# Loading 384 depthwise weights straight to their partitions, and the first two supertiles' transposes and stores in another order

## The chip, the cores and the metric

The kernel runs on one core of one Trainium2 chip. The metric is the device time of one execution in microseconds; the time before is 574.61 us, the median of 7 runs (574.41 to 575.1). A NeuronCore has engines with instruction streams of their own: TensorE (PE in the profile, with PEld for the loading of the stationary operand), VectorE (DVE), ScalarE (ACT), GpSimd (POOL) and SyncE (SP), which here only issues DMAs. Sixteen DMA engines move data between HBM and the on-chip SBUF. Engines wait for each other, and for DMAs, by semaphores.

## The reference

With k = 1 the depthwise part is a scaling of each of the 384 channels, and the pointwise part a 384 x 384 matrix product on each of the 384 x 384 pixels:

```python
xp = jnp.pad(x, ((0,0),(pad,pad),(pad,pad),(0,0)))       # pad = 0
for i in range(k):
    for j in range(k):
        out = out + xp[:, i:i+H, j:j+W, :] * dw[i, j][None, None, None, :]
return jnp.einsum('bhwc,cd->bhwd', out, pw)
```

Inputs and output are bf16: x is (1, 384, 384, 384), dw (1, 1, 384), pw (384, 384). 147,456 pixels of 768 bytes are read and as many written.

## The kernel before

The scaling is folded into the matrix: row c of pw is multiplied by dw[c] once, and then out = x times the scaled matrix. A supertile is 512 pixels, and there are 288 of them. They are loaded in chunks: 1, 1, 2, 2 and 4 supertiles (group 0), then groups of 10, and smaller chunks again at the end. Three X buffers and three O buffers hold a group each and are used in turn.

For each supertile VectorE makes two transposes (L349, halves h = 0 and 1) of 32 x 32 blocks of pairs of bf16, from X into T. TensorE multiplies (L211): 48 matmuls in 12 steps of four, one for each group of 32 rows of the array, into one of two PSUM halves PS[0], PS[1]. ScalarE copies PSUM to O as bf16 (L406), and SP stores O. T, PS and O are guarded by the semaphores s_t, s_pe, s_a and s_o. TensorE runs the supertiles in a hardware loop (L270); the last supertile has code of its own.

Before the loop the scaled matrix w_r is made in the layout that the transposes leave. Each step of it has a line:

- ScalarE's queue loads dw as one row in one partition (L166, dw_row). SP's queue loads pw in two DMAs (L167, L168), and then x: the chunks of group 0, then groups 1 and 2 (L128). Group 1's load is issued after supertile 1's has landed.
- TensorE works on constants meanwhile (`idle_work`, L228: four groups of four matmuls, and two more groups after dw). Three small matmuls (L241) turn dw_row into a column for each third of the channels, in PSUM; VectorE copies them to dw_f (L374).
- GpSimd makes an identity matrix, VectorE adds it up to a selection matrix sel (L367), and multiplies sel by each column of dw_f (L377), which gives sel_w for k = 0, 1, 2.
- TensorE multiplies sel_w with pw (L261), six results (k, r); it waits for the first pw DMA, for the second at k = 1, and for each sel_w. The results are copied to w_r (L362): number 1 by VectorE, the others by ScalarE in order.
- The first matmul of the loop waits for number 1, for ScalarE's first three casts and for the first transpose; two later steps of the first supertile wait for the fourth and the fifth cast (`w_first`).
- On VectorE the order is: sel, dw_f, the three sel_w, its cast of w_r, the four transposes of supertiles 0 and 1, and then the loop, in which the transposes of supertile jj + 2 follow the eviction of jj.

SP's stream is a list sorted by due times (`todo`): a load of a group that reuses an X buffer is due after the last supertile of the group that had it, and a store one place after the supertile it ends with. Each group-0 chunk has one store. Ahead of the very first store stand 28 waits that are already satisfied (L183). A store waits for ScalarE's copy, then its DMA is issued (L161). ScalarE waits for the stores of a group before its O buffer is written again (L390).

The transposes write T by the pattern below, so that the word at place i*4 + k of T is row i of block k. The pixel of output partition p is then p itself, and a chunk's store writes, for each of the four row groups q, L*768 contiguous bytes a partition.

```python
Tw = Ts[s][:].bitcast(U32).rearrange("p b (i k) -> p b k i", k=4)
```

Of the kernel before, what the change touches and what calls it, by code (L numbers as in the profile page):

```python
# [7 lines left out]
BF16 = mybir.dt.bfloat16  # L8
F32 = mybir.dt.float32
U32 = mybir.dt.uint32  # L10
# [3 lines left out]
NR = 3  # L14
LONG_AT = [8, 148]
PARTS = [slice(0, 4, 2), slice(1, 2), slice(3, 4)]
# [11 lines left out]
def kernel(  # L28
# [12 lines left out]
    nc = tc.nc  # L41
    P = nc.NUM_PARTITIONS
    B, H, W, C = x.shape
    assert dw.shape[0] == 1 and dw.shape[1] == 1, "only k=1 depthwise supported"
    D = pw.shape[1]
# [7 lines left out]
    NS = N // 512  # L53
    groups = _groups(NS)

    chunks, first = [], 0
# [2 lines left out]
            chunks.append((g, i, sum(ls[:i]), first, L))  # L59
            first += L  # L60
    NT = len(chunks)
    n_parts = [1 if c[0] + 1 < len(groups) else len(PARTS) if c[3] + 1 == NS else 2 for c in chunks]
    g_end = [max(c[3] + c[4] for c in chunks if c[0] == g) - 1 for g in range(len(groups))]

    consts = ctx.enter_context(tc.tile_pool(name="consts", bufs=1))
# [7 lines left out]
    eye = consts.tile([P, P], BF16, name="eye")  # L73
    sel = consts.tile([P, 2, 32], F32, name="sel")
    w_r = consts.tile([P, NB, 2, D], BF16, name="w_r")
    dw_row = consts.tile([1, C], BF16, name="dw_row")
    dw_f = consts.tile([P, 3], F32, name="dw_f")
    warm = consts.tile([P, 2], F32, name="warm")

    ones = nc.const_aps.tensor(1.0, [P, D], BF16)  # L80
# [17 lines left out]
    s_dw = nc.alloc_semaphore("s_dw")  # L98
    s_pw = nc.alloc_semaphore("s_pw")
    s_pw2 = nc.alloc_semaphore("s_pw2")  # L100
    s_df = nc.alloc_semaphore("s_df")
    s_sw = nc.alloc_semaphore("s_sw")
    s_dwf = nc.alloc_semaphore("s_dwf")
    s_sel = nc.alloc_semaphore("s_sel")
# [3 lines left out]
    with tc.tile_critical(sync_engine=mybir.EngineType.Pool, no_gpsimd_drain=True):  # L108
# [25 lines left out]
        def store(t, k):  # L134
            g, i, off, first, L = chunks[t]
            je = first + L * (k + 1) // n_parts[t] - 1
            src = Os[g % NR][:, 4 * off * D : 4 * (off + L) * D]
            rows = of[512 * first : 512 * (first + L), :]
            if first + 2 < NS:
                dst = rows.rearrange("(q p j) d -> p q (j d)", q=4, p=P)  # L140
                src = src.rearrange("p (q e) -> p q e", q=4)
                e = L * D // n_parts[t]
                dst, src = dst[:, :, e * k : e * k + e], src[:, :, e * k : e * k + e]
                nc.sync.wait_ge(s_a[je % 2], je // 2 + 2)
            elif first + 2 == NS:
                dst = rows.rearrange("(m q) d -> m (q d)", q=4)
                part = slice(2 * D * k, 2 * D * k + 2 * D)
                dst, src = dst[:, part], src[:, part]
                nc.sync.wait_ge(*((s_a[0], NS // 2 + 1) if k == 0 else (s_d, 1)))
            else:  # L150
                dst = rows.rearrange("(m p) d -> p m d", p=P)[:, PARTS[k], :]
                src = src.rearrange("p (m d) -> p m d", d=D)[:, PARTS[k], :]
                if k == 0:
                    nc.sync.wait_ge(s_d, 2)
                    nc.sync.wait_ge(s_a[1], NS // 2 + 1)
                elif k == 1:
                    nc.sync.wait_ge(s_d, 3)
                else:
                    nc.scalar.wait_ge(s_a[1], NS // 2 + 2)
            eng = nc.scalar if first + 1 == NS and k == 2 else nc.sync  # L160
            eng.dma_start(dst, src).then_inc(s_o[g % NR], 16)  # L161
# [1 line left out]
        w_eng = [1, 0, 1, 1, 1, 1]  # L163
        w_all = [(s_wr[e], w_eng.count(e)) for e in range(2)]

        nc.scalar.dma_start(dw_row[:], dw.rearrange("a e c -> a (e c)")).then_inc(s_dw, 16)  # L166
        nc.sync.dma_start(pw_n[:, 0], pw[0:P, :]).then_inc(s_pw, 16)  # L167
        nc.sync.dma_start(pw_n[:, 1:3], pw[P:C, :].rearrange("(k p) d -> p k d", p=P)).then_inc(s_pw2, 16)  # L168
        load_x(0)
# [7 lines left out]
        for _, f, a in sorted(todo, key=lambda a: a[0]):  # L177
            if f is load_x and chunks[a[0]][4] == LMAX and chunks[a[0]][0] == 1:
                nc.sync.wait_ge(x_of(1)[1], 16)
            if f is store and a[0] == 0:  # L180

                for _ in range(28):
                    nc.sync.wait_ge(s_pw, 16)  # L183
            f(*a)
# [40 lines left out]
        def idle_work(n):  # L225
            for _ in range(n):
                for i in range(4):
                    nc.tensor.matmul(  # L228
                        PS[0][:, 2 * (i % 2) + i // 2, :D],
                        lhsT=ones[32 * i : 32 * i + 32, 0:P],  # L230
                        rhs=ones[32 * i : 32 * i + 32, :],
                        start=True,
                        stop=True,
                        tile_position=(32 * i, 0),
                    )

        idle_work(4)

        nc.tensor.wait_ge(s_dw, 16)
        for k in range(3):  # L240
            mm = nc.tensor.matmul(  # L241
                PS[1][:, 0, D + k : D + k + 1],
                lhsT=dw_row[:, P * k : P * k + P],
                rhs=ones[0:1, 0:1],
                start=True,
                stop=True,
            )
        mm.then_inc(s_df)
        idle_work(2)
        nc.tensor.wait_ge(s_pw, 16)  # L250
        times = {(2, 0): 2, (2, 1): 2}
        for k in range(3):
# [77 lines left out]
        def transposes(t, j):  # L330
            g, i, off, first, L = chunks[t]
            jj = first + j
            s = jj % 2
            if jj + 1 == NS:
                nc.vector.wait_ge(s_xk, 32)
                Tw = Ts[s][:].bitcast(U32).rearrange("p (v j) (m w) -> p v j m w", v=2, m=4)
                Xw = Xk[:].bitcast(U32).rearrange("p (j v m) w -> p v j m w", v=2, m=4)
                for v in range(2):
                    ins = nc.vector.transpose(out=Tw[:, v], in_=Xw[:, v])  # L339
                    ins._wait_ge(s_pe, 2 * (jj - 2) + v + 1)  # L340
                    ins.then_inc(s_t[s][v])
                return
            X, sem, n = x_of(t)
            Xw = X.bitcast(U32).rearrange("p (k l) c -> p k l c", l=L)
            Tw = Ts[s][:].bitcast(U32).rearrange("p b (i k) -> p b k i", k=4)
            for h in range(2):
                if h == 0 and j == 0:
                    nc.vector.wait_ge(sem, n)
                ins = nc.vector.transpose(  # L349
                    out=Tw[:, 3 * h : 3 * h + 3],  # L350
                    in_=Xw[:, :, j, 96 * h : 96 * h + 96].rearrange("p k (b w) -> p b k w", w=32),
                )
                if jj >= 2:
                    ins._wait_ge(s_pe, 2 * (jj - 2) + h + 1)
                ins.then_inc(s_t[s][h])

        order = [(t, j) for t in range(NT) for j in range(chunks[t][4])]

# [11 lines left out]
            op=mybir.AluOpType.add,  # L370
            axis=mybir.AxisListType.X,
        ).then_inc(s_dwf)
        nc.vector.wait_ge(s_df, 1)
        nc.vector.tensor_copy(dw_f[:], PS[1][:, 0, D : D + 3]).then_inc(s_dwf)  # L374
        nc.vector.wait_ge(s_dwf, 2)
        for k in range(3):
            nc.vector.tensor_scalar_mul(  # L377
                sel_w[:, k], sel[:].unsqueeze(2).to_broadcast([P, 2, 4, 32]), dw_f[:, k : k + 1]
            ).then_inc(s_sw)
        for i in range(6):  # L380
            w_out(i)
# [3 lines left out]
        for jj, (t, j) in enumerate(order):  # L385
            g, i, off, first, L = chunks[t]
            s = jj % 2
            Ov = Os[g % NR][:, 4 * off * D : 4 * (off + L) * D].rearrange("p (q j d) -> p q j d", q=4, d=D)
            if j == 0 and i == 0 and g >= NR:
                nc.scalar.wait_ge(s_o[g % NR], 16 * sum(map(len, groups[g % NR : g : NR])))  # L390
            if jj + 2 == NS:
                nc.vector.wait_ge(s_pe, 2 * jj + 2)
                nc.vector.wait_ge(s_o[g % NR], 16 * sum(map(len, groups[g % NR : g : NR])))
                a = nc.scalar.copy(Ov[:, 0:2, j, :], PS[s][:, 0:2, :D])  # L394
                a._wait_ge(s_pe, 2 * jj + 2)
                a.then_inc(s_a[s])
                nc.vector.tensor_copy(Ov[:, 2:4, j, :], PS[s][:, 2:4, :D]).then_inc(s_d)  # L397
                continue
            if jj + 1 == NS:
                for n, m in enumerate((0, 2, 1, 3)):  # L400
                    o = (nc.scalar.copy if n % 2 else nc.vector.tensor_copy)(Ov[:, m, j, :], PS[s][:, m, :D])  # L401
                    o._wait_ge(s_pe, 2 * jj + 1 + n)
                    o.then_inc(s_a[s] if n % 2 else s_d)
                store(t, 2)
                continue
            a = nc.scalar.copy(Ov[:, :, j, :], PS[s][:, :, :D])  # L406
            a._wait_ge(s_pe, 2 * jj + 2)
            a.then_inc(s_a[s])

            if jj == LONG_AT[0]:  # L410
                load_last(nc.scalar)
            if jj == LONG_AT[1]:
                nc.scalar.wait_ge(s_xk, 32)
                load_x(NT - 2, nc.scalar)
            if jj + 2 < NS:
                transposes(*order[jj + 2])
# [30 lines left out]
```

## Time and profile before

| What | Value |
|---|---|
| median of 7 runs | 574.61 us |
| the profiled execution's own time | 574.66 us |
| its span in the profile | 572.4 us |
| TensorE busy | 566.4 us (99%) |
| VectorE busy | 506.4 us (88%) |
| ScalarE busy | 418.5 us (73%) |
| DMA, mean over the span | 396 GB/s |
| first matmul of the loop (L211) | 6.54 us |
| end of the loop's matmuls | 566.38 us |

Times in the profile count from the start of the span. A line of the timeline has the start, the length, the engine, the line of the kernel, the operation, what it writes and reads, how many instructions are merged into it, and in brackets how long the engine was idle before and what ended that. A wait for several semaphores is put down to one of them, the one that the profile takes to have come last. The loop's matmuls run four at a time, so that their lengths overlap.

### The profile page before, as it was taken

How to read it: one execution, taken by the hardware profiler on the slowest of the kernel's cores; microseconds unless marked ns; L12 is line 12 of the kernel's file. 1: busy time of each engine (PE TensorE's matmuls, PEld its weight loads, DVE VectorE, ACT ScalarE, POOL GpSimd, SP SyncE). 2: the span in 40 equal slices, each digit the busy share in tenths (PEclk: the TensorE clock that was granted, in tenths of full speed). 3: DMA queues.
4: the chain of work that ended last, by engine and by line, in shares of the span. 5: the costliest groups of instructions: out<-in, count | busy, mean ns of one | idle time of the engine just before them, and what ended most of it. 6: DMA issues, size and time to landing. Idle time of an engine off the chain costs nothing.

```text
span 572.4 us, 29681 instructions
## 1 busy us (share of the span) xinstructions
PE 566.4 (99%) x13835; PEld 419.5 (73%) x13835; DVE 506.4 (88%) x585; ACT 418.5 (73%) x297; POOL 17.0 (3%) x45
## 2 busy tenths in 40 slices
PE   8999999999999999999999999999999999999997
PEld 4777777777777777777777777777777777777774
DVE  7889889889889889889888988988988988988985
ACT  6777777777777777777777777777777777777775
POOL 4042000000000000000000000000000000000000
PEclk9999999999999999999999999999999999999999
DMA  8999999999999999999999999999999999999677
GB/s 335 439 387 424 421 421 426 440 419 418 426 418 420 382 397 430 401 379 398 425 389 392 414 421 389 412 413 421 410 383 428 401 391 394 422 394 379 256 289 251
DMA packets 26896, 226.88 MB, mean 396 GB/s; under 512 B 1285, under 2 KB 7558, under 8 KB 23046
## 3 DMA queue, kind: packets, MB, share of 16 engines
q1 hardware_dynamic: 25696, 225.91, 97.4%
q10 hardware_dynamic: 1190, 0.89, 0.5%
q14 instruction: 9, 0.07, 0.0%
q8 instruction: 1, 0.02, 0.0%
HBM read 113.54 MB, written 113.25 MB: 396 GB/s over the span
## 4 chain that ended last, share of the span: by engine, by line
PE 98%; DMA 1%; DVE 0%; SPq 0%; issue 0%; ACT 0%; POOLq 0%
PE ps L211 98%; DMA X<-in_x_dram 1%; PE ps L279 0%; DVE T L349 0%; ACT O L401 0%; SPq L168 0%; SPq L167 0%; SPq L442 0%; POOLq L108 0%; POOLq L431 0%
## 5 line engine op out<-in xcount | busy, mean ns | idle before, releaser
L211 PE MATMUL ps<-w_r,T 32*128 32x384 bf16 x13776 | 559.8, 321 | 0.8 <-DVE T L349 0.8
L349 DVE STREAM_TRANSPOSE T<-X 128x384 uint32<-128x384 uint32 x572 | 499.2, 876 | 57.1 <-DMA X<-in_x_dram 2.1
L211 PEld LDWEIGHTS ps<-w_r,T 32*128 32x128 bf16 x13776 | 417.2, 93 | 143.4 <-issue 1.2
L406 ACT CAST O<-ps 128x1536 bf16<-128x1536 f32 x286 | 411.6, 1439 | 146.8 <-PE ps L211 146.8
L326 POOL COPY Xk<-Xl 32x256 bf16<-32x256 bf16 (+1 forms) x32 | 10.1, 341 | 22.7 <-DMA Xl<-in_x_dram 21.9
L316 POOL COPY raw<-w_r 32x768 bf16<-32x768 bf16 x8 | 6.4, 821 | 6.5 <-ACT w_r L362 6.3
L362 ACT CAST w_r<-ps 128x768 bf16<-128x768 f32 x5 | 3.7, 810 | 0.8 <-PE ps L261 0.8
L228 PE MATMUL ps<-const-bfloat16-1.0 32*128 32x384 bf16 x24 | 2.2, 516 | 1.1 <-PEq L431 1.1
L261 PE MATMUL ps<-raw 64*128 64x384 bf16 x16 | 2.2, 374 | 0.2
L328 ACT ACT_TABLE_LOAD x1 | 1.3, 1283 | 1.5 <-PEq L431 1.5
L279 PE MATMUL ps<-raw,T 64*128 64x384 bf16 (+1 forms) x16 | 2.2, 326 | 0.0
L397 DVE CAST O<-ps 128x768 bf16<-128x768 f32 x1 | 1.0, 956 | 1.4 <-PE ps L211 1.4
L261 PEld LDWEIGHTS ps<-raw 64*128 64x128 bf16 x16 | 0.5, 99 | 2.2 <-DMA raw<-in_pw_dram 1.5
L349 DVE STREAM_TRANSPOSE T<-Xl 128x384 uint32<-128x384 uint32 x2 | 1.8, 877 | 0.2
L279 PEld LDWEIGHTS ps<-raw,T 64*128 64x128 bf16 (+1 forms) x16 | 1.0, 96 | 1.2 <-issue 0.6
L228 PEld LDWEIGHTS ps<-const-bfloat16-1.0 32*128 32x128 bf16 x24 | 0.7, 117 | 1.4 <-issue 1.4
L401 ACT CAST O<-ps 128x384 bf16<-128x384 f32 x2 | 1.0, 479 | 0.9 <-PE ps L279 0.9
L339 DVE STREAM_TRANSPOSE T<-Xk 128x384 uint32<-128x384 uint32 x2 | 1.2, 578 | 0.5 <-PE ps L211 0.4
L367 DVE TENSOR_REDUCE sel<-eye 128x64 f32<-128x128 bf16 x1 | 0.3, 287 | 1.5 <-POOL eye L302 1.5
L401 DVE CAST O<-ps 128x384 bf16<-128x384 f32 x2 | 1.1, 558 | 0.3 <-PE ps L279 0.2
L362 DVE CAST w_r<-ps 128x768 bf16<-128x768 f32 x1 | 1.0, 958 | 0.5 <-PE ps L261 0.5
L394 ACT CAST O<-ps 128x768 bf16<-128x768 f32 x1 | 0.8, 799 | 0.5 <-PE ps L211 0.5
(10 smaller groups left out, 2.5 us busy)
## 6 DMA issues: line engine op xcount, KB each, us to landing
X<-in_x_dram SPq DMA_DIRECT2D x26, 3840.0 KB, 22.0
out_dram<-O SPq DMA_DIRECT2D x26, 3840.0 KB, 28.0
X<-in_x_dram SPq DMA_DIRECT2D x3, 1536.0 KB, 18.8
out_dram<-O SPq DMA_DIRECT2D x4, 768.0 KB, 9.4
out_dram<-O SPq DMA_DIRECT2D x2, 1536.0 KB, 14.1
X<-in_x_dram SPq DMA_DIRECT2D x3, 768.0 KB, 7.5
X<-in_x_dram SPq DMA_DIRECT2D x1, 2304.0 KB, 20.4
out_dram<-O SPq DMA_DIRECT2D x1, 2304.0 KB, 12.2
```

Of the source, the lines that this page charges most:

```text
L211: mm = nc.tensor.matmul(PS[s][:, q, :D], lhsT=Ts[s][32 * q : 32 * q + 32, b, par::2], rhs=w_r[32 * q : 32 * q + 32, b, par, :], start=(b, ...
L228: nc.tensor.matmul(PS[0][:, 2 * (i % 2) + i // 2, :D], lhsT=ones[32 * i : 32 * i + 32, 0:P], rhs=ones[32 * i : 32 * i + 32, :], start=True ...
L261: mm = nc.tensor.matmul(PS[(k + 1) % 2][:, 2 * r + v, :D], lhsT=sel_w[64 * v : 64 * v + 64, k, r, :, :].rearrange("p q w -> p (q w)"), rhs ...
L279: return nc.tensor.matmul(PS[1][:, m, :D], lhsT=Tk[rows, at : at + P, par], rhs=w_k[rows, k, par, :], start=start, stop=stop, tile_positio ...
L316: nc.gpsimd.tensor_copy(w_k[rows, k], w_r[rows, b]).then_inc(s_wk)
L326: nc.gpsimd.tensor_copy(dst, src).then_inc(s_xk)
L328: nc.scalar.copy(warm[:, s : s + 1], nc.const_aps.tensor(0.0, [P, 1], F32)).then_inc(s_a[s])
L339: ins = nc.vector.transpose(out=Tw[:, v], in_=Xw[:, v])
L349: ins = nc.vector.transpose(out=Tw[:, 3 * h : 3 * h + 3], in_=Xw[:, :, j, 96 * h : 96 * h + 96].rearrange("p k (b w) -> p b k w", w=32),)
L362: o = nc.vector.tensor_copy(out, in_) if e == 0 else nc.scalar.copy(out, in_)
L401: o = (nc.scalar.copy if n % 2 else nc.vector.tensor_copy)(Ov[:, m, j, :], PS[s][:, m, :D])
L406: a = nc.scalar.copy(Ov[:, :, j, :], PS[s][:, :, :D])
```

## The change

dw is loaded by a DMA of 384 packets of two bytes, from ScalarE's queue as before, to 128 partitions of three elements (dw_c). The row, the three matmuls, dw_f and their semaphore go; sel_w is now a product of two tensors, sel and dw_c, and VectorE waits for the DMA itself. TensorE's work on constants is five groups in one piece in place of four and two.

The first two chunks, one supertile each, are transposed so that T holds the 32 words of a block k in a run. Output partition p = 32k + i then holds pixel 4i + k of each row group q, so each of these two chunks is stored by four DMAs of 32 partitions. The number of stores in a group enters the waits for O buffers, which are now counted from `n_parts`.

```diff
-    n_parts = [1 if c[0] + 1 < len(groups) else len(PARTS) if c[3] + 1 == NS else 2 for c in chunks]
+    n_parts = [(4 if t < 2 else 1) if c[0] + 1 < len(groups) else len(PARTS) if c[3] + 1 == NS else 2 for t, c in enumerate(chunks)]
...
-    dw_row = consts.tile([1, C], BF16, name="dw_row")
-    dw_f = consts.tile([P, 3], F32, name="dw_f")
+    dw_c = consts.tile([P, 3], BF16, name="dw_c")
...
-            if first + 2 < NS:
+            if t < 2:
+                dst = rows.rearrange("(q i k) d -> k i q d", q=4, k=4)[k]
+                src = src[32 * k : 32 * k + 32].rearrange("p (q d) -> p q d", q=4)
+                if k == 0:
+                    nc.sync.wait_ge(s_a[first % 2], first // 2 + 2)
+            elif first + 2 < NS:
...
-        nc.scalar.dma_start(dw_row[:], dw.rearrange("a e c -> a (e c)")).then_inc(s_dw, 16)
+        with nc.allow_non_contiguous_dma(reason="dw to partitions"):
+            nc.scalar.dma_start(dw_c[:], dw.rearrange("a e (k p) -> p (a e k)", p=P)).then_inc(s_dw, 16)
...
-            if f is store and a[0] == 0:
+            if f is store and a == (0, 0):
...
-        idle_work(4)
-
-        nc.tensor.wait_ge(s_dw, 16)
-        for k in range(3):
-            mm = nc.tensor.matmul(
-                PS[1][:, 0, D + k : D + k + 1],
-                lhsT=dw_row[:, P * k : P * k + P],
-                rhs=ones[0:1, 0:1],
-                start=True,
-                stop=True,
-            )
-        mm.then_inc(s_df)
-        idle_work(2)
+        idle_work(5)
...
-            Tw = Ts[s][:].bitcast(U32).rearrange("p b (i k) -> p b k i", k=4)
+            Tw = Ts[s][:].bitcast(U32).rearrange(
+                "p b (k i) -> p b k i" if t < 2 else "p b (i k) -> p b k i", k=4
+            )
...
+        def o_free(g):
+            return 16 * sum(n_parts[t] for t, c in enumerate(chunks) if c[0] < g and c[0] % NR == g % NR)
...
-        nc.vector.wait_ge(s_df, 1)
-        nc.vector.tensor_copy(dw_f[:], PS[1][:, 0, D : D + 3]).then_inc(s_dwf)
-        nc.vector.wait_ge(s_dwf, 2)
+        nc.vector.wait_ge(s_dwf, 1)
+        nc.vector.wait_ge(s_dw, 16)
         for k in range(3):
-            nc.vector.tensor_scalar_mul(
-                sel_w[:, k], sel[:].unsqueeze(2).to_broadcast([P, 2, 4, 32]), dw_f[:, k : k + 1]
+            nc.vector.tensor_tensor(
+                out=sel_w[:, k],
+                in0=sel[:].unsqueeze(2).to_broadcast([P, 2, 4, 32]),
+                in1=dw_c[:, k : k + 1].unsqueeze(2).unsqueeze(3).to_broadcast([P, 2, 4, 32]),
+                op=mybir.AluOpType.mult,
             ).then_inc(s_sw)
...
-                nc.scalar.wait_ge(s_o[g % NR], 16 * sum(map(len, groups[g % NR : g : NR])))
+                nc.scalar.wait_ge(s_o[g % NR], o_free(g))
```

More of the change, by code (lines that the diff above doesn't have):

```diff
@@ L100 @@
     s_pw2 = nc.alloc_semaphore("s_pw2")
-    s_df = nc.alloc_semaphore("s_df")
     s_sw = nc.alloc_semaphore("s_sw")
@@ L389 @@
             if j == 0 and i == 0 and g >= NR:
-                nc.scalar.wait_ge(s_o[g % NR], 16 * sum(map(len, groups[g % NR : g : NR])))
+                nc.scalar.wait_ge(s_o[g % NR], o_free(g))
             if jj + 2 == NS:
                 nc.vector.wait_ge(s_pe, 2 * jj + 2)
-                nc.vector.wait_ge(s_o[g % NR], 16 * sum(map(len, groups[g % NR : g : NR])))
+                nc.vector.wait_ge(s_o[g % NR], o_free(g))
                 a = nc.scalar.copy(Ov[:, 0:2, j, :], PS[s][:, 0:2, :D])
```

## The prediction

> **What bounds the kernel now.** I read the page first, then the chain that ended last, then the timeline of the first 13 us, then the waits of the DMA queue SP.
>
> The page's first part and its chain by engine:
>
> ```profile
> span 572.4 us, 29681 instructions
> PE 566.4 (99%) x13835; PEld 419.5 (73%) x13835; DVE 506.4 (88%) x585; ACT 418.5 (73%) x297; POOL 17.0 (3%) x45
> ...
> PE 98%; DMA 1%; DVE 0%; SPq 0%; issue 0%; ACT 0%; POOLq 0%
> ```
>
> TensorE is busy 99% of the span and carries 98% of the chain. The chain in order of time says where the rest lies:
>
> ```profile
> 1.87 3.69 DMA X<-in_x_dram
> 5.56 0.02 issue
> 5.59 0.87 DVE T L349
> 6.45 0.09 issue
> 6.54 559.83 PE ps L211 x13776
> ```
>
> From 6.54 us on there is one unbroken run of matmuls: 287 supertiles in 559.83 us, 1.951 us each. Nothing in the change touches a matmul of L211, so the change can move the end in two ways only: it moves the start at 6.54 us, or it makes the run stall. Two chains meet at that start, and the timeline of the first microseconds shows both:
>
> ```profile
> 0.97 0.54 ACTq L166 DMA_DIRECT2D dw_row<-in_dw_dram  x1
> ...
> 2.31 0.21 PEld L241 LDWEIGHTS ps<-const-bfloat16-1.0,dw_row 1*128 1x128 bf16 x2 [0.41 <-DMA dw_row<-in_dw_dram]
> ...
> 2.67 0.16 DVE L374 COPY dw_f<-ps 128x3 f32<-128x3 f32 x1 [0.91 <-PE ps L241]
> ...
> 2.87 0.88 DVE L377 TENSOR_SCALAR raw<-sel,dw_f 128x256 bf16<-128x256 f32 x3
> 3.34 0.16 PEld L261 LDWEIGHTS ps<-raw 64*128 64x128 bf16 x4 [0.74 <-DMA raw<-in_pw_dram]
> ...
> 3.91 3.67 ACT L362 CAST w_r<-ps 128x768 bf16<-128x768 f32 x5 [0.79 <-PE ps L261]
> ...
> 4.26 0.13 PEld L261 LDWEIGHTS ps<-raw 64*128 64x128 bf16 x4 [0.77 <-DMA raw<-in_pw_dram]
> ...
> 5.59 2.95 DVE L349 STREAM_TRANSPOSE T<-X 128x384 uint32<-128x384 uint32 x4 [0.40 <-DMA X<-in_x_dram]
> ```
>
> The data chain: x lands at 5.57, the first transpose ends at 6.45, matmuls start at 6.54. The weight chain: dw lands at 2.27, three tiny matmuls and a copy turn it, sel_w is ready from 3.22 (2.87 plus one L377 of 0.35), L261 starts at 3.34, ScalarE casts from 3.91. The wait at 3.34 is labelled with pw, but pw's first block landed 2.0 us after its issue at 0.96, so at about 3.0; the late one is sel_w. The first supertile needs ScalarE's third cast. It begins at 5.36 and lasts 0.80: 6.17. In the semaphore records TensorE passes the weights at 6.21 and T at 6.49. So the data chain decides, and the weight chain has 0.28 us to spare. Its middle is also held by the second pw block: landed 4.22, seen at 4.26, 0.40 later the second cast.
>
> **The change part by part, against the profiled execution's own time of 574.66 us (0.05 over the median 574.61 of the runs shown).**
>
> *Transposes of supertiles 0 and 1 in contiguous runs.* L349 writes with a stride of four words and takes 0.86 us; L339 at the end of the kernel moves the same 128x384 words in contiguous runs and takes 0.578. I take that row: 0.28 us off each of four transposes. Only the first is on the path: the data chain is ready at 6.545 - 0.28 = 6.27. Bounds: 0 (the runs don't matter) and 0.28. When this goes, the weights are late next: third cast 6.17 plus the same 0.10 to the matmul is 6.27 as well. No more than 0.28 us can be won, and only with unchanged weights.
>
> *dw straight to partitions.* Removed: three L241 matmuls, the L374 copy and two semaphore hops, 2.27 to 2.87. Added: the L377 products become tensor-tensor operations of the same 256 elements; I price them at L377's own 0.35 each (bounds 0.29, the reduction at L367, and 0.58, the contiguous transpose of 384). VectorE now waits for dw itself; behind that wait stand sel_w, one cast of w_r and the first transposes, so a late dw delays all of them and, through sel_w, TensorE and ScalarE. With dw landing at D: product starts D+0.03, ends D+0.38; L261 starts 0.12 later, at D+0.50; the first cast follows 0.57 later (3.34 to 3.91), at D+1.07; ScalarE's casts follow each other at 0.69 to 0.70 (4.67, 5.36), so the third ends 2.19 after the first begins, at D+3.26; plus 0.10, matmuls start at D+3.36. Against 6.545 that breaks even at D = 3.19.
>
> What is D? Before, one packet of 768 B landed 1.30 us after the issue at 0.97. Now 384 packets of 2 B, 24 for each of 16 DMA engines. No row has such a packet. From below: the trace's 4-byte semaphore packets take 9 ns, 24 of them 0.2 us, so D = 2.5. From above: pw's second block, 16 packets per engine of 768 B, landed 1.2 us after the first block, 76 ns a packet; 24 of those are 1.8 us, D = 4.1; and if pw's own 24 packets per engine (36 ns each in the packet records, 0.86 us) come in between, D = 4.95. They will: dw stays on ScalarE's queue, pw and x are on SP's, and at 32 to 33 us, where both queues carry 768 B packets, the records show 159 of the one to 144 of the other, one for one. I take 48 packets of 36 ns from the first packet at 1.94, which is 3.67, plus 0.2 for the landing: D = 3.85. That is near the row of equal packet count, and takes 2 B as no cheaper than 768 B. Then matmuls start at 7.21.
>
> The Trainium skill (DMA: Bandwidth & Descriptors, Specifications) speaks against this edit: under 512 B a DMA engine does a read-modify-write. No row here shows one. As an estimate, if that doubled each packet's 36 ns, D would be 4.7 and the total 576.2; the number below does without it.
>
> *What dw's packets take from the others.* At most 24 x 36 ns = 0.86 us of each DMA engine before x. Between 2 and 3.5 us the engines are half idle (129 to 369 GB/s in the slices of the DMA view there), so I put half on x and pw: x lands at about 6.0, data chain 6.7; pw's second block 4.65, weights 6.7 by that limb. Both are below 7.21. Bounds 0 and 0.86: even 0.86 gives 7.13.
>
> *Idle matmuls, 24 to 20.* Nothing waits for them; they end near 2.9 where sel_w now comes at 4.2. The gap matters only for the clock (rival below).
>
> *Stores of supertiles 0 and 1, 2 DMAs to 8.* Six more issues on SP at 0.40 (10.26 and 12.14 took that), 2.4 us between 10.3 and 13.8, while SP otherwise waits for ScalarE. Queued behind: the next store, whose issue hangs anyway,
>
> ```profile
> 16.04 17.22 SPq L161 DMA_DIRECT2D out_dram<-O  x2
> ...
> 33.30 1.38 SPq L128 DMA_DIRECT2D X<-in_x_dram  x1
> ```
>
> and the x load of group 3, issued at 33.30 and landed at 50.4, first needed at 6.54 + 28 x 1.951 = 61.2. I cost this at nothing; its cover is 10.8 us on the load and, for the O buffers of group 0 (last landing 54.2, wanted at 67), 12.8. Even if each quarter took as long as a whole store did in the queue (1.0 us for the first, 1.9 for the second), that would be 3 x 2.9 = 8.7 us. The tightest place elsewhere is group 1's load: VectorE sees it at 24.35, its transpose ends 25.29, TensorE wants it at 26.04. A delay of x by 0.43 against a start later by 0.67 loosens that.
>
> *Sum.* 7.21 - 6.545 = +0.67 on 574.66: 575.3 in a profiled execution, and about the same against the median, 574.61 + 0.67 = 575.3. A change under 0.2%, 1.15 us, is about what a measurement of this kernel can't tell from none.
>
> **The rivals.**
>
> *A. dw lands early, not slower.* If small packets are nearer 9 ns than 36, D stays at or below 3.19 and the contiguous transposes count: 574.66 - 0.28 = 574.4. For it: 768 B packets keep the engines half idle at 2 to 3.5 us, so there is room. Against: D must beat a load that needed 3.26 us for the same packet count.
>
> *B. dw packets cost more than 768 B ones.* From D = 4.33 on the loss exceeds 1.15 us. At D = 4.95 it is 8.31 - 6.545 = 1.77: 576.4. For it: one packet per element, 24 deep on each engine. Against: the same packets would then delay pw, which the estimate already holds.
>
> *C. The clock comes late.* L228's matmuls take 0.52 us, as do the first of L261; at 4.27 they take 0.36, later 0.32: full speed is granted near 4.35, after 3.2 us of almost unbroken work. Now TensorE idles from 2.9 to 4.35. If the grant comes one such stretch later, at 7.7, L261 and 0.5 us of L211 run at about half speed: +0.6 on top, 575.9. If two later, some 4 us of L211 do, +2: 577.3. Against: a gap of 0.8 us before 6.54 costs no clock.
>
> The Trainium skill (TensorE: Matmul & The Clock Gate, Part 1) gives a free-running window of about 3.4 us whose activity decides the clock; it leaves open how much work in it is enough, so it allows both, and the run will show.
>
> *D. The stores bite.* If the eight small stores held SP or the queue more than 10.8 us longer, group 3 would come late; with double my upper 8.7 that is a stall of 6.6: about 582.
>
> **How the numbers follow.** The likeliest, dw between 3.19 and 4.33: 0.40; A 0.18; B 0.23; C 0.13; D 0.06. Predicted is the likeliest's 575.3; its own range is 574.6 to 575.8. The range for 8 in 10 takes in A's 574.3 and all but the far ends of B and C: 574.3 to 576.8. Slower by over 0.2%: all of B, 0.12 of C, 0.05 of D and 0.01 of the edge, 0.41. Faster by over 0.2% would need matmuls at 5.4, before x lands at 5.57: 0.02 for what I don't see. The same: 0.57.
>
> **What would show it.** In the changed kernel: four transposes near 0.58; the products' start, which is D; L261 0.47 after it; the matmul run starting 3.33 after the products' start and lasting 559.8. If the wait before L211 is on T and not on w_r, A is right. If L261 after 4.4 still shows 0.52, C. If a stall of VectorE on X appears near 61, D. I am wrong if the run starts outside 6.2 to 8.8, or lasts longer than before.

## The result and the profile after

The changed kernel takes 576.44 us, the median of 14 runs (575.59 to 577.0), against 574.61 (34 runs): slower by the ratio 1.0028, 95% interval [1.0021, 1.0035]. The profiled execution took 576.31 us with a span of 574.1, so 1.65 us over the profiled execution of before.

The page's first lines and the chain by engine:

```profile
span 574.1 us, 29673 instructions
PE 567.6 (99%) x13828; PEld 357.1 (62%) x13828; DVE 507.1 (88%) x584; ACT 418.5 (73%) x297; POOL 17.0 (3%) x45
...
PE 99%; DMA 1%; issue 0%; ACT 0%; DVE 0%; POOLq 0%; ACTq 0%; DVEq 0%
```

TensorE is the bound as before. The chain that ended last, in order of time (start, length, what), shows what now stands ahead of the run of matmuls:

```profile
0.97 2.92 DMA dw_c<-in_dw_dram
...
3.99 0.44 DVE raw L373
4.43 0.14 issue
4.56 1.46 PE ps L253 x8
6.03 0.02 issue
6.05 1.47 PE ps L253 x8
7.51 560.71 PE ps L215 x13181
```

Before, this chain began with x and the first transpose. Now it begins with dw, which lands 2.92 us after its issue, and runs through the products and the making of w_r. The timeline of the first microseconds has the same steps and one thing that the chain hides:

```profile
3.99 1.09 DVE L373 TENSOR_TENSOR raw<-sel,dw_c 128x256 bf16<-128x256 f32 x3 [2.23 <-DMA dw_c<-in_dw_dram]
...
4.56 2.95 PE L253 MATMUL ps<-raw 64*128 64x384 bf16 x16 [1.66 <-DVE raw L373]
...
5.10 3.61 ACT L359 CAST w_r<-ps 128x768 bf16<-128x768 f32 x5 [2.05 <-PE ps L253]
...
7.45 5.83 PE L215 MATMUL ps<-w_r,T 32*128 32x384 bf16 x116
...
9.02 0.16 PEld L215 LDWEIGHTS ps<-w_r,T 32*128 32x128 bf16 x4 [0.16 <-issue]
9.34 3.71 PEld L215 LDWEIGHTS ps<-w_r,T 32*128 32x128 bf16 x92 [0.16 <-issue]
```

The first matmul of the loop starts at 7.45 us, 0.91 later than before. And up to 9.34 TensorE loads four weights every 0.32 us; from there on the loads follow without a break. That is the moment when full speed is granted; the trace's clock record has it at 9.40, where before it was 4.35, ahead of the loop. The loop's matmuls last 560.77 us from the first start to the last end, against 559.83. So 0.91 of late start and 0.94 of slow start make 1.84 at the last matmul (568.22 against 566.38), of which the span shows 1.6, since the part behind the last matmul is 0.2 shorter in this execution.

The waits of SP's queue show the load of group 3 and the stores:

```profile
12.10 21.84 SPq L164 DMA_DIRECT2D out_dram<-O  x10
33.98 1.98 SPq L126 DMA_DIRECT2D X<-in_x_dram  x1
```

The ten stores fill the time in which SP hung before anyway, and group 3's load is issued at 33.98 in place of 33.30. It lands at 51.8 and is wanted near 62; VectorE waits for no x after group 0's chunks.

### The profile page after: what moved, and what is told of

Same layout as the page of the kernel before. It is cut to its first block, busy times and chain, and to the rows that moved or that the text cites. A ratio compares the mean times of both kernels' runs of the same rounds, so it can differ in the third digit from the quotient of the medians.

```text
span 574.1 us, 29673 instructions
## 1 busy us (share of the span) xinstructions
PE 567.6 (99%) x13828; PEld 357.1 (62%) x13828; DVE 507.1 (88%) x584; ACT 418.5 (73%) x297; POOL 17.0 (3%) x45
## 4 chain that ended last, share of the span: by engine, by line
PE 99%; DMA 1%; issue 0%; ACT 0%; DVE 0%; POOLq 0%; ACTq 0%; DVEq 0%
PE ps L215 98%; PE ps L253 1%; DMA dw_c<-in_dw_dram 1%; PE ps L271 0%; ACT O L400 0%; DVE raw L373 0%; ACTq L441 0%; POOLq L106 0%; DVEq L371 0%; POOLq L430 0%
## 5 line engine op out<-in xcount | busy, mean ns | idle before, releaser
L215 PEld LDWEIGHTS ps<-w_r,T 32*128 32x128 bf16 x13776 | 354.6, 93 | 206.4 <-issue 1.6
L253 PE MATMUL ps<-raw 64*128 64x384 bf16 x16 | 2.9, 513 | 1.7 <-DVE raw L373 1.7
L253 PEld LDWEIGHTS ps<-raw 64*128 64x128 bf16 x16 | 0.9, 113 | 3.7 <-issue 3.0
```

Of the source, the lines that this page charges most:

```text
L215: mm = nc.tensor.matmul(PS[s][:, q, :D], lhsT=Ts[s][32 * q : 32 * q + 32, b, par::2], rhs=w_r[32 * q : 32 * q + 32, b, par, :], start=(b, ...
L253: mm = nc.tensor.matmul(PS[(k + 1) % 2][:, 2 * r + v, :D], lhsT=sel_w[64 * v : 64 * v + 64, k, r, :, :].rearrange("p q w -> p (q w)"), rhs ...
```

## The experiments

After the result the theory was: the late dw packets delay the weights (0.91 us), the gap in TensorE's work that they leave delays the clock (0.94), and the stores and transposes cost nothing. Rivals: the stores or transposes carry part of it; the clock moves by itself; and, later, several theories on why dw is late. In all runs the head of the kernel was read from the profile, since the times of one kernel spread by 1 to 4 us and their medians alone tell little. The table has, from each trace, when dw, pw's second block and the first x land, the loop's first matmul, the clock's grant (the moment from which the trace shows full speed) and the length of the run of matmuls, and the fastest of the timed runs (the medians are in the text).

| kernel | dw | pw 2nd | x | start | grant | run | fastest |
|---|---|---|---|---|---|---|---|
| before | 2.27 | 4.22 | 5.56 | 6.54 | 4.35 | 559.83 | 574.26 |
| changed | 3.89 | 4.93 | 5.94 | 7.45 | 9.40 | 560.77 | 575.59 |
| e1, dw as a row | 2.24 | 3.97 | 5.45 | 6.25 | 6.65 | 560.00 | 574.21 |
| e2, dw part alone | 3.79 | 4.76 | 5.92 | 7.35 | 9.81 | 561.02 | 575.52 |
| e3, gap filled | 3.92 | 4.74 | 5.84 | 7.48 | 6.92 | 559.83 | 575.29 |
| e4, before with a gap | 2.27 | 3.90 | 5.71 | 6.70 | 7.99 | 560.44 | 574.70 |
| e5, packets unused | 2.55 | 3.94 | 6.42 | 7.41 | 4.61 | 559.83 | 575.20 |
| e6, stores alone | 2.24 | 4.55 | 5.89 | 6.87 | 10.25 | 561.47 | 574.30 |
| e7, a third of dw | 4.02 | 4.86 | 6.06 | 7.58 | 7.82 | 559.93 | 575.44 |
| e8, e1 again | 2.51 | 3.87 | 5.49 | 6.41 | 5.94 | 559.83 | 574.14 |
| e9, 128 x 768 B | 3.41 | 3.96 | 6.19 | 6.97 | 7.64 | 560.14 | 574.91 |
| e10, on SP's queue | 3.61 | 4.80 | 6.55 | 7.25 | 8.22 | 560.28 | 575.39 |
| e11, 128 x 2 B, spread | 3.17 | 5.14 | 6.14 | 7.37 | 10.51 | 561.35 | 574.71 |
| e12, 384 x 2 B, spread | 3.66 | 4.48 | 5.59 | 7.22 | 9.36 | 560.86 | 574.92 |

**e1 and e8: dw as a row, the rest of the change kept.**

```diff
-            nc.scalar.dma_start(dw_c[:], dw.rearrange("a e (k p) -> p (a e k)", p=P)).then_inc(s_dw, 16)
+        nc.scalar.dma_start(dw_row[:], dw.rearrange("a e c -> a (e c)")).then_inc(s_dw, 16)
...
-        idle_work(5)
+        idle_work(4)
+
+        nc.tensor.wait_ge(s_dw, 16)
...
+        mm.then_inc(s_df)
+        idle_work(2)
```

The three small matmuls, the copy to dw_f and the products with a scalar for each partition come back with it.

> The changed kernel with dw loaded as one row again (row, three small matmuls, copy, and the old idle matmuls); contiguous transposes and stores in parts stay. Theory (late dw packets, and through them a late TensorE clock, make the whole loss): the first matmul of the loop at 6.27 us in place of 6.54, the run of matmuls 559.8 us long, time 574.3 (0.28 below before). Rival (the eight stores or the contiguous transposes cost something themselves): 574.9 or more, with the run of matmuls longer than 559.9 or a start after 6.6.

The start came at 6.25, near the expected 6.27, but the weights set it: the first transpose was done at 6.05, as x had landed 0.11 earlier than before, and the third cast at 6.11. Median 574.70 against 574.83 on that chip, ratio 1.0005 [0.999, 1.0019]. The run of matmuls was 560.00 in place of 559.8, because the clock was granted at 6.65, 0.4 after the start.

> The same kernel as in the first run with dw as one row (contiguous transposes, stores in parts), now beside the others on this chip, since the runs of the first comparison lay far apart. Theory: start 6.2 to 6.3 us, 0.1 to 0.3 us under before. Rival (stores or transposes cost something): at or over before.

Median 574.61 against 574.92, ratio 0.9988 [0.9975, 1.0002]. The start was 6.41: the row landed 0.24 later than before, and the chain goes through ScalarE's casts:

```profile
4.06 2.21 ACT w_r L372 x3
6.28 0.14 issue
6.41 559.83 PE ps L216 x13776
```

What is left of the change without the packets costs nothing. Its start is 0.13 to 0.29 us earlier in the two traces, 0.08 to 0.11 of that by an earlier x, and that is too small for either interval: neither is clear of 1. This is the best version of the study, level with the kernel before as far as the times tell.

**e2: the dw part alone.** The kernel before with dw_c, the products of two tensors and `idle_work(5)`; old transposes and stores.

> The kernel before with the dw part of the change alone (2-byte packets to partitions, product of two tensors, 20 idle matmuls); transposes and stores as before. Theory: weights decide the start, so the transposes don't matter: start at 7.4 to 7.5 us, clock granted around 9, time 576.2 to 576.6, the same as the changed kernel. Rival (stores or transposes carry part of the loss): 575.5 or less.

Start 7.35, grant 9.81, median 576.16 (ratio 1.0011 [0.9996, 1.0025] on a chip where the runs of before reached 578.6); the profiled execution took 576.48. The head repeats that of the changed kernel to 0.1 us in the landing and in the start, and the fastest run 575.52 its 575.59. With e1 and e8 the traces show that the late start and the late clock come with dw's part of the change; by the times alone e2 would not show it, as its interval takes in 1.

**e3: the gap filled.**

```diff
-        idle_work(5)
+        idle_work(10)
```

> The changed kernel with 40 idle matmuls in place of 20, so that TensorE works from 1.1 us until dw's products are there. Theory (half of the loss is the clock, which came at 9.4 us because TensorE idled from 2.9 to 4.56): clock granted at 4.3 to 4.6 as before, L261 at full speed, start near 7.0, run of matmuls 559.8 long, time 575.0 (1.4 under the changed kernel, 0.4 over before), and runs that agree more closely than the 575.6 to 577.0 of the changed kernel. Rival (the late packets alone make the loss and the clock moves by itself): clock late again, 576.4.

Half right. The run of matmuls is back at 559.83, since the clock was granted at 6.92, ahead of the start. It did not come at 4.35, since the stretch up to 3.51 had begun at 0.10, before TensorE's work did, and held 2.39 us (such stretches are explained at e4). But the start stayed at 7.48: L253 still ran at the slow clock until 6.92, and full speed would have won little, because ScalarE's casts follow each other at 0.69 us (5.13, 5.83, 6.52) at either clock. Only the first cast would have come earlier, by some 0.17, as a pair of L253 takes 0.50 slow and 0.33 at full speed. The profiled execution took 575.65, 0.66 under the changed kernel's. The median, 576.15 (ratio 1.0017 [1.0007, 1.0028]), does not show the gain, and the runs spread as far as without the filling; why is open.

**e4: before, with a gap.** `idle_work(4)` becomes `idle_work(2)` and the second `idle_work(2)` goes.

> The kernel before with 8 idle matmuls in place of 24, so that TensorE is idle most of 1.8 to 3.3 us; dw, transposes and stores as before. Theory (a gap in TensorE's work delays the clock by itself, without any DMA): clock granted 3 to 5 us later than 4.35, start at 6.5 to 6.7, run of matmuls 1.0 to 1.5 us longer, time 575.6 to 576.2. Rival (the clock does not depend on this gap): 574.6, as before.

Grant 7.99, start 6.70, run 560.44; median 575.72 against 574.83 (ratio 1.0007 [0.9997, 1.0017], so not clear of 1 by the times). In the trace the gap alone costs 0.61 us of the run, less than the 1.0 to 1.5 expected, without any DMA being changed. The start is 0.16 later because x landed 0.15 later.

What decides the grant can be read from TensorE's busy time in the stretch of 3.41 us that ends with the grant, and in the one before it (columns: stretch, its length, busy time and matmuls, clock, DMA share, GB/s; the clock column says 1.00 here because the trace has no record before the grant). The kernel before, with the stretch after its grant as well, e4, the changed kernel, and e6 and e8:

```profile
0.94:4.35 3.41, 3.08 (x33) 1.00 0.61 166
4.35:7.76 3.41, 2.54 (x44) 1.00 1.04 387
```

```profile
1.17:4.58 3.41, 2.31 (x19) 1.00 0.65 174
4.58:7.99 3.41, 2.94 (x30) 1.00 1.03 396
```

```profile
2.57:5.99 3.42, 1.76 (x16) 1.00 0.87 248
5.99:9.40 3.41, 3.39 (x38) 1.00 0.99 411
```

```profile
3.42:6.84 3.42, 2.88 (x16) 1.00 0.97 333
6.84:10.25 3.41, 3.38 (x44) 1.00 1.04 432
```

```profile
2.53:5.94 3.41, 3.32 (x30) 1.00 0.96 301
```

In the fourteen traces every stretch ahead of the grant with 2.94 us of work or more, as the profile models it, got the clock, and none with 2.88 or less did. Once it was granted, 2.54 us in the next stretch did not lose it again. In the changed kernel the stretch that ended at 5.99 held 1.76 us: the end of the idle matmuls and the beginning of L253, with the wait for dw between them. The closest comparison is e8, where dw comes as a row and the old idle matmuls are back: its stretch lies within 0.05 us of that one, held 3.32, and got the clock at 5.94, ahead of the loop. The loop loses half of the time from its start to the grant: (9.40 - 7.45)/2 = 0.98, measured 0.94; e2 1.23 and 1.19; e4 0.64 and 0.61; e6 1.69 and 1.64; e11 1.57 and 1.52; nothing where the grant came first. Where the stretches lie differs from execution to execution, which moves the loss; the spread of the changed kernel's runs, 575.6 to 577.0, is what that would give, but this is argued, as those runs have no trace.

The Trainium skill (TensorE: Matmul & The Clock Gate, Part 1) says that the window is 3413 ns, runs freely and needs sustained work. The traces agree: from the grant to the withdrawal at the end are 566.61 us before and 563.20 after, 166.0 and 165.0 windows of 3.4133.

**e6: the stores alone.** Four DMAs of 32 partitions for each of the first two supertiles, rows in the old order, transposes and dw as before.

> The kernel before with the first two supertiles stored by four DMAs of 32 partitions each, rows in the old order; dw and transposes as before. Theory (the stores are hidden): start at 6.5 to 6.6 us, run of matmuls as long as the clock's grant allows (559.8 plus half of what the grant is later than the start), time within 0.3 us of before; group 3's load issued up to 2 us later. Rival (eight stores cost something): 0.5 us or more over before, with a stall in the run of matmuls.

Median 574.88 against 574.92, ratio 0.9992 [0.998, 1.0005]: the stores cost nothing. Group 3's load is issued at 34.13. The profiled execution, though, took 576.41: in it pw's second block landed at 4.55, TensorE waited for it from 4.2 to 4.6, the stretch up to 6.84, which that wait and a shorter one ahead of the loop fell into, held 2.88 us and the clock came at 10.25. So the head of the kernel before can lose 1.6 us to the clock as well, by a DMA that is 0.3 us late.

**e5: the packets loaded, and not used.** The kernel before, and right behind the row's DMA the load of dw_c, which nothing reads.

> The kernel before, with the 384 packets of 2 bytes loaded besides (ScalarE's queue, right after the row) into a tile that nothing reads. Theory (the packets hold up pw and x as well, whoever waits for them): pw's second block lands at 4.7 to 5.0 us in place of 3.9 to 4.2, x at 5.8 to 6.0, start at 6.8 to 7.0, time 575.0 plus whatever a late clock adds. Rival (the packets cost only the one who waits for them, VectorE): pw's second block at 3.9 to 4.3, start at 6.5 to 6.7, time as before, 574.6.

Median 576.92 against 574.92, ratio 1.0025 [1.0011, 1.0039]. The packets cost others, but not whom I expected: pw's second block came at 3.94, on time, and x at 6.42, against 5.45 to 5.89 in the five kernels without the packets. The chain runs through x:

```profile
1.87 4.55 DMA X<-in_x_dram
...
6.44 0.87 DVE T L354
...
7.41 559.83 PE ps L216 x13776
```

Here the packets were issued 0.57 us later than in the changed kernel, so they met x rather than pw. This execution took 575.41; what makes the median 2.0 us longer than before has no trace.

**e7: a third of dw.** 128 packets in place of 384.

```diff
-            nc.scalar.dma_start(dw_c[:], dw.rearrange("a e (k p) -> p (a e k)", p=P)).then_inc(s_dw, 16)
+            nc.scalar.dma_start(dw_c[:, 0:1], dw.rearrange("a e (k p) -> p (a e k)", p=P)[:, 0:1]).then_inc(s_dw, 16)
...
-                in1=dw_c[:, k : k + 1].unsqueeze(2).unsqueeze(3).to_broadcast([P, 2, 4, 32]),
+                in1=dw_c[:, 0:1].unsqueeze(2).unsqueeze(3).to_broadcast([P, 2, 4, 32]),
```

> The changed kernel with the first third of dw alone loaded, 128 packets of 2 bytes in place of 384, and used for all channels (so two thirds of the channels are scaled by the wrong weights). Theory (the landing goes by the number of packets, 24 for each DMA engine, some 50 ns each): dw lands at 2.9 to 3.1 us in place of 3.9, pw's second block at 4.2 to 4.4, start at 6.3 to 6.6, time 574.4 to 574.8. Rival (a scattered load has a fixed cost whatever its count): dw at 3.7 or later, start 7.2 to 7.5, 575.5 to 576.5.

My theory fell here. dw landed at 4.02, no earlier than with three times as many packets:

```profile
0.97 3.05 DMA dw_c<-in_dw_dram
```

All 12 runs took 575.44 us or more (median 575.80, ratio 1.0008 [0.9997, 1.002]). In the packet records a 2-byte packet takes 7 to 9 ns, so 24 of them are 0.2 us of a DMA engine. The time lies between the packets: in the changed kernel they begin from 2.28 to 3.53 us, and the sixteen increments of the semaphore come one after another from 3.00 to 3.89. Three explanations were left: small packets land late (S); a load over all 16 engines lands late beside pw's on the other queue (Q); all 16 engines read the same few hundred bytes (H).

**e9: 128 packets of 768 B.** The load becomes `dma_start(dw_c[:], pw[0:P, :])`, with dw_c 384 wide.

> The changed kernel with dw's load replaced, on the same queue and place, by 128 packets of 768 B (the first 128 rows of pw), whose first three columns stand in for dw (so the channels are scaled by the wrong weights). It has the count of the load of a third of dw, another size, and another source for every partition. Theory S (2-byte packets land late for their size) and theory H (all 16 DMA engines read the same 768 bytes): lands at 3.0 to 3.3 us, products start there, fastest runs 574.8 or less. Theory Q (any load spread over the 16 engines lands late beside pw's loads on the other queue): 3.7 to 4.2 us, fastest runs 575.3 or more.

3.41 us: between the two expectations, so it doesn't decide. Median 575.92, ratio 1.0017 [1.0006, 1.0027], fastest 574.91.

**e10: the 2-byte load first on SP's queue.** `nc.scalar.dma_start` becomes `nc.sync.dma_start` at the same place.

> The changed kernel with the same 384 packets of 2 bytes issued first on SP's queue, ahead of pw and x, in place of ScalarE's. Theory Q: with one queue nothing interleaves, dw lands at 2.7 to 3.2 us, and pw and x come 0.4 to 0.8 later for the issue and the packets ahead of them. Theories S and H: dw lands at 3.4 to 4.0 us as before, since size and source are the same, and pw and x wait behind it.

dw at 3.61, pw and x behind it at 4.80 and 6.55; median 576.28, ratio 1.0019 [1.0006, 1.0032]. With one queue the load still takes 2.65 us from its issue, and its increments come from 2.86 to 3.61. Q falls as the main cause; some 0.3 us may be the other queue's.

**e11: 128 packets of 2 bytes from 128 places.** The load becomes `dma_start(dw_c[:, 0:1], pw[0:P, 0:1])`, 768 B apart.

> The changed kernel with 128 packets of 2 bytes as in the load of a third of dw, but read from 128 rows of pw, 768 B apart, in place of 256 adjacent bytes (one column scales all channels, so the scaling is by the wrong weights). Theory H (16 engines read the same few hundred bytes): lands at 3.2 us or earlier. Theories S and Q: 3.7 to 4.2 us, as with adjacent bytes.

To be set beside e7: same count, same size, same queue, another source. The timelines of e7 and of e11 (VectorE's products, which start when dw is there):

```profile
4.11 1.10 DVE L373 TENSOR_TENSOR raw<-sel,dw_c 128x256 bf16<-128x256 f32 x3 [2.35 <-DMA dw_c<-in_dw_dram]
```

```profile
3.26 1.10 DVE L373 TENSOR_TENSOR raw<-sel,dw_c 128x256 bf16<-128x256 f32 x3 [1.50 <-DMA dw_c<-in_pw_dram]
```

dw lands at 3.17 in place of 4.02, the 16 engines within 0.32 us of each other, and earlier than the 128 packets of 768 B. Five of the twelve runs lie below e7's fastest, 575.44, and the fastest took 574.71. S and Q fall. The median, 575.53, is only 0.27 under e7's. (This execution started at 7.37 for another reason: one engine brought pw's second block at 5.14, the other fifteen by 3.89.)

**e12: 384 packets of 2 bytes from 384 places.** Three columns, 256 bytes apart, of 128 rows of pw.

> The changed kernel with all 384 packets of 2 bytes, each read from another place: three columns, 256 bytes apart, of 128 rows of pw, in place of 768 adjacent bytes (the scaling is by the wrong weights). Theory H (late because 16 engines read the same few hundred bytes): lands at 3.2 to 3.5 us, fastest run 575.0 or less, like the 128 spread packets (3.17 us, 574.71). Rival N (384 packets are late by their number too): 3.7 to 4.0 us, fastest run 575.3 or more.

Fifteen of the 16 engines were done by 3.25 and one at 3.66, where with adjacent bytes they came evenly up to 3.89. The landing, 3.66, lies between the two expectations; the fastest run, 574.92, fits H, but the other eleven took 576.0 or more, and the median, 576.71 (ratio 1.0032 [1.0022, 1.0042]), does not fit it.

So for 128 packets the source makes 0.85 us, in one trace of each and borne out by the fastest runs. What of the source it is has not been separated: e7 reads adjacent elements of dw, e11 elements at the start of rows of pw, so the spacing, the addresses at which the reads start and the tensor differ together, and no run reads adjacent elements of pw. Against dw being slow to reach in itself stands its row, which landed 1.30 us after its issue; and in e5, where that row had just been read, the increments of the packets still came one after another from 3.82 to 5.24. For 384 the engines' spread points the same way as for 128, but how much is the number and how much the source stays open, as does why reads of the same bytes should wait for one another.

## Why the prediction was right, and where it wasn't

The measured 576.44 lies in the range given (574.3 to 576.8) and on the side of slower by over 0.2%, which had 0.41 against 0.57 for the same; the likeliest case's 575.3 was 1.1 us too low. What came is rival C's case, a landing near the likeliest one's and a late clock on top, and C had 0.13. Most of the 0.41 stood on B, and that B's 576.4, from a D of 4.95 and no late clock, is near the measured total is luck.

- *What bounds the kernel, and that only the start or a stall can move the end.* Right. Both moved.
- *D = 3.85.* It landed at 3.89, but not for the reason worked out, so the nearness is luck. The step "48 packets of 36 ns" assumed that dw's packets are as long as pw's and that their number counts. They take 7 to 9 ns, and a third of them lands no earlier (e7). Where 128 packets are read from made 0.85 us, between one trace and another.
- *The Trainium skill's rule on packets under 512 B* (DMA: Bandwidth & Descriptors, Specifications: read-modify-write). No run shows a price of it: 128 spread packets of 2 B landed at 3.17, 128 of 768 B at 3.41.
- *Start at 7.21, D+3.36.* It was 7.45, and 3.56 after the landing; e2, e3, e7, e9 and e12 have the same 3.56. The landing gave 0.04 of the 0.24. The first product began 0.10 after the landing in place of 0.03, behind two waits of VectorE, and took 0.425 in place of 0.35, which gives 0.07 each; the rest is within a few hundredths a step.
- *x at 6.0 and pw's second block at 4.65.* 5.94 and 4.93. That they are held up was right, and e5 shows it for x alone.
- *Transposes at 0.58, data chain 6.27 without the packets.* 0.567 and 0.534. As argued, the weights are late next: they set the start in e1, 6.25, and in e8, 6.41. So e1's 6.25 does not show the data chain's 6.27; there the data were ready by 6.14, with x 0.11 earlier.
- *Stores at nothing.* Right (e6), with SP's hanging issue as the cover.
- *"Idle matmuls: nothing waits for them", and the run of matmuls 559.8.* The step that failed. The gap between 2.9 and 4.56 cost the clock, and that 0.94 us was named as rival C with 0.13 and left out of the likeliest sum. Its price was right in kind (half of the time that the loop runs slow); the grant came at 9.40, between one stretch later (7.7) and two (about 11). C's sign was there, L253's matmuls at 0.47 to 0.52 to the end, and so was the one of being wrong, a run of matmuls longer than before (560.77). Its counter-argument, that the gap of 0.8 us before 6.54 costs no clock, was no evidence: in that trace the clock had been granted at 4.35, and the stretch with that gap kept it with 2.54 us of work, where a grant took 2.94. A late clock should have had most of the chance and a place in the sum: in the seven traces with dw's load to partitions and no filling the run is 0.10 to 1.52 us longer than 559.83, by 0.79 on average.

## What to carry to other kernels

A wait in the first microseconds can be paid twice when TensorE idles in it: once as a later start, and again as a later clock, since in these traces the clock was granted only for a window that was nearly full of work (2.94 us of 3.41). Before a scattered load replaces a contiguous one with work behind it, look at what else the start waits for: here the old path of row, three small matmuls and a copy ended at 2.87 and was off the chain, so that by the measured 3.56 from landing to start only a landing before 2.98 could have helped. The earliest landing of any load to partitions here was 3.17. And a landing read in one trace is one sample; in the five kernels without the packets the same loads moved by 0.3 to 0.7 us.

## What was not expected of the hardware

- 128 packets of 2 bytes landed 2.2 us after their issue when read 768 B apart from pw, and 3.05 us when read from 256 adjacent bytes of dw, in one trace each. The packets themselves take 7 to 9 ns.
- The clock was granted for every window with 2.94 us or more of TensorE work in 3.41, and for none with 2.88 or less; once granted, it was kept through a window with 2.54.
- The product of sel with a broadcast column of bf16 takes 0.42 us as an operation of two tensors, 0.35 as one with a scalar for each partition; the next starts 0.34 later in place of 0.27.
- A transpose on VectorE that writes runs of 32 words takes 0.53 to 0.58 us, one that writes every fourth word 0.83 to 0.88.
